# GpSimd's arithmetic in the chunk steps moves to VectorE, and the later blocks of T are placed by DMA

## The chip, the cores and the metric

The kernel runs on one core of a Trainium2 chip. Five engines work side by side, each with its own instruction queue: TensorE (PE in the profile, its weight loads PEld), VectorE (DVE), ScalarE (ACT), GpSimd (POOL) and SyncE (SP), which here only issues DMAs. The metric is the device time of one execution in microseconds (us); lower is better. The kernel before takes 1076.54 us, the median of three runs (1076.4 to 1076.81).

## The reference

The input goes through three layers. The first is a delta-rule attention over 768 tokens for 4 batches of 8 heads with a head size of 48. For each token

```
y[t]   = q[t] @ state
state += beta[t] * outer(k_n[t], v[t] - k_n[t] @ state)        # k_n = k / (|k| + 1e-6)
```

The second is a mixture of 8 experts (384 to 1024 to 384, ReLU). Each of the 3072 tokens goes to the expert with the largest gate logit and is scaled by its softmax weight and by a sigmoid gate. The third is a gated layer, (sigmoid(x @ w_gate) * (x @ w_val)) @ w_out with a width of 1536. Every layer needs the whole output of the one before.

## The kernel before

The attention works on chunks of 32 tokens. A chunk of all 32 pairs of batch and head is one step, so there are 24 steps (`NSTEP`), numbered s. Four steps form a group g (s4 = s % 4), two steps a pair u (s2 = s % 2). The recurrence inside a chunk is solved with a triangular inverse T, one 32x32 matrix for each batch, head and chunk.

A step in program order, with the tiles that the profile names:

1. `KS` = K · state (32 matmuls) on TensorE, then VectorE makes `W` = scaled V minus KS (line 780). `Y` = Q · state follows `KS` on TensorE (line 796).
2. `U` = T · W, 32 matmuls that read `TBD` (line 805). ScalarE rounds `U` to float16 (`UH[:,0]`, line 807), VectorE subtracts to get the low part (`UH[:,1]`, line 811).
3. TensorE fills the time until `UH` is there with the transpose of an earlier output (`XTP`) and with the Gram and Q·K products of step s + 11 (`GP`; up to step 12), then updates the state (`Sps`, 48 matmuls, line 844: high·high, low·high, high·low), and ScalarE copies it to `SH` for the next step's `KS`.
4. TensorE adds the part of the output inside the chunk (`Y` from `PBD`, line 849), the gate logits (`GL`) and the rest of `GP`.

Work for later steps runs beside it. `KH` is the normalised K of a later pair as float16 high and low part (`kh_mul` and `kh_split_hi` on ScalarE, `kh_split_lo` on GpSimd), which four DMAs place in `KBD` (`kexp`). `P` is the masked Q·K product of a later pair: `p_split` scales it and masks it on GpSimd, ScalarE rounds it (`p_split_hi`), GpSimd subtracts for the low part (`p_split_lo`), and four DMAs place it in `PBD` (`expand`). `v_mul` scales V on GpSimd. T of group g + 1 is made while group g runs: `prep` makes norms and the scaled Gram matrix `Lt` (two multiplications over 128x1024 on GpSimd in `scale`, line 341), `inv_ops` runs 31 columns of a multiplication (`tmp<-X,Lt`) and an addition (`X<-X,tmp`) on VectorE, a share of which GpSimd takes (`tmpG`, rows from `SHE[g]` on; `share_rows`). `last` turns X into `XT`, and `expand_t` copies it into `TBD`: the block of step s4 = 0 at once, the blocks of the three later steps in step s4 = 0 of the group, two by VectorE behind the low part of `UH`, two by ScalarE (lines 379 to 385, 813, 874).

Each engine's instructions run in the order of the program text; inside the attention the class `Queue` chains them so. Where the work for later steps goes on VectorE is set by `Filler`: it holds VectorE's side work as pieces with an estimated duration and issues pieces up to a budget at two places of a step: `TA` (2.4) between `W` and the low part of `UH`, and `TB` (4.2; `TC` = 3.8 from step 12 on) at the end of a step. At the end of a group, lines 910 to 912 issue whatever of the next T is still missing, ahead of the next `W`.

GpSimd also scatters each step's tokens to their experts by an indirect DMA (`scatter`). SyncE's queue holds, per step, the loads of later K, Q and V and the four-DMA placements.

Of the kernel before, what the change touches and what calls it, by code (L numbers as in the profile page):

```python
# [7 lines left out]
F32 = mybir.dt.float32  # L8
# [5 lines left out]
ALU = mybir.AluOpType  # L14
# [7 lines left out]
NSTEP, NG = SEQ // CH, SEQ // CH // 4  # L22
# [12 lines left out]
LA = 11  # L35
# [9 lines left out]
XE = (0, 1, 2, 3, 4, 5)  # L45
TB0 = 3.5
# [1 line left out]
WG = 2.7  # L48
WP = 4.5
WE = 1.0  # L50
TC = 3.8
NR = 8
Q2 = 0.0
GS = 6
KA = 1
SHE = (0, 32, 24, 20, 20, 20)
TA = 2.4
TB = 4.2
W0 = 36
YS = 69  # L60
QS = 11
# [34 lines left out]
GAP = 0.12  # L96


class Filler:
# [26 lines left out]
    def run(self, budget):  # L126
        self.t = max(self.t, self.until)
        self.until += budget
        while (self.main or self.chains) and self.t < self.until:
            self.step()  # L130

    def flush(self, chain):
        while chain[1]:
            self.step()
# [6 lines left out]
class Attention:  # L141
# [5 lines left out]
    def run(self, small, acc, zero_fill, small_loads):  # L147
# [42 lines left out]
            return ins.ins  # L190

        def load_kth(u):
            t = wk.tile([128, 2, 48, 8], F32, tag="kth", name="kth", bufs=1)
            SP.dma_start(out=t.rearrange("p s d h -> p s (d h)"), in_=a["ktok"][:, 2 * u : 2 * u + 2])
            KTOK[u] = t

# [2 lines left out]
            SP.dma_start(out=t, in_=a["vtok"][:, 2 * u : 2 * u + 2])  # L199
            VT[u] = t  # L200

        def v_mul(s):
            g, s4 = divmod(s, 4)
            v = VT[s // 2][:, s % 2].rearrange("p (h e) -> p h e", h=8)
            G.tensor_tensor(out=v, in0=v, in1=nt[:, g, 8 * s4 : 8 * s4 + 8].unsqueeze(2).to_broadcast([128, 8, 48]), op=ALU.mult)


        GPS = {}
# [64 lines left out]

        PMS = {}

        def p_split(u):
            g, i = divmod(u, 2)
            if g:
                pm = GPM[g][1][:, 16 * i : 16 * i + 16]
                G.tensor_tensor(out=pm, in0=pm, in1=rnt[:, g, 16 * i : 16 * i + 16].unsqueeze(2).to_broadcast([128, 16, 32]), op=ALU.mult)  # L280
            else:
                pm = PM.pop(u)
            G.tensor_tensor(out=pm, in0=pm, in1=mask.unsqueeze(1).to_broadcast([128, 16, 32]), op=ALU.mult)
# [6 lines left out]
        def p_split_lo(u):  # L290
            G.tensor_tensor(out=PHL[u][:, 1], in0=PMS.pop(u), in1=PHL[u][:, 0], op=ALU.subtract)

        def expand(dst, src):
            for b in range(4):
# [1 line left out]


        def kh_mul(u, half=None):
            r = rnt[:, u // 2].rearrange("p (s h) -> p s h", s=4)
            for i in (range(2) if half is None else (half,)):  # L300
                kt = KTOK[u][:, i]
                if u == 0 or KA:
                    for h in range(8):
                        A.activation(out=kt[:, :, h], in_=kt[:, :, h], func=AF.Copy, scale=r[:, 2 * (u % 2) + i, h : h + 1])
                    continue
                G.tensor_tensor(out=kt, in0=kt, in1=r[:, 2 * (u % 2) + i].unsqueeze(1).to_broadcast([128, 48, 8]), op=ALU.mult)
# [6 lines left out]
                A.copy(out=KH[:, s, 0], in_=by_head(KTOK[u][:, s]))  # L313
            KHG[u] = KH

        def kh_split_lo(u):
            KH, src = KHG[u], KTOK.pop(u)
            for s in range(2):
                G.tensor_tensor(out=KH[:, s, 1], in0=by_head(src[:, s]), in1=KH[:, s, 0], op=ALU.subtract)


        def kexp(u):
# [7 lines left out]
        def prep(g):  # L330
            Lt = ep.tile([128, 32, 32], F32, tag="Lt", name="Lt", bufs=2)
            L1 = Lt.rearrange("p c a -> p (c a)")
            x, y, t, q = [ep.tile([128, 32], F32, tag=n, name=n, bufs=1) for n in ("bx", "by", "bt", "bq")]
            LT[g] = Lt
            R = R0 if g < 2 else R2
            tt = lambda o, a, b: (0.1, GAP, lambda: V.tensor_tensor(out=o, in0=a, in1=b, op=ALU.mult))
            ts = lambda o, a, s1, s2, op1=ALU.add: (0.085, GAP, lambda: V.tensor_scalar(out=o, in0=a, scalar1=s1, scalar2=s2, op0=ALU.mult, op1=op1))
            st = lambda o, a, s1, b, op0=ALU.add: (0.1, GAP, lambda: V.scalar_tensor_tensor(out=o, in0=a, scalar=s1, in1=b, op0=op0, op1=ALU.mult))
            tr = lambda o, i, d: (d, 0.0, lambda: V.transpose(out=o, in_=i))

            def scale(E, j0, j1, i0):
                L = Lt[:, j0:j1, i0:]
                E.tensor_tensor(out=L, in0=L, in1=x[:, j0:j1].unsqueeze(2).to_broadcast([128, j1 - j0, 32 - i0]), op=ALU.mult)
                E.tensor_tensor(out=L, in0=L, in1=nbr[:, g, i0:].unsqueeze(1).to_broadcast([128, j1 - j0, 32 - i0]), op=ALU.mult)


            ops = [
                (1.135, GAP, lambda: V.transpose(out=L1, in_=GPM[g][0].rearrange("p b c -> p c b"))),
                (0.085, GAP, lambda: V.tensor_scalar_max(out=x, in0=L1[:, 0:1024:33], scalar1=1e-36)),
                ts(y.bitcast(I32), x.bitcast(I32), -0.5, 1595932665.0),  # L350
                tt(t, y, y),
                tt(t, t, x),
                st(y, t, -2.38924456, y),
                tt(t, y, y),
                tt(t, t, x),
                ts(q, t, 0.375 * RS**4, -1.25 * RS**2),
                tt(q, q, t),
                st(y, q, 1.875, y),
                tt(y, y, x),
                ts(y, y, -RS / KSC, 1e-6 / KSC),  # L360
                (0.27, GAP, lambda: V.reciprocal(out=x, in_=y)),
                st(nbr[:, g], x, -1.0 / (KSC * KSC), be[:, g], ALU.mult),
                tr(rnt[:, g], x, 0.1),
                tr(nt[:, g], y, 0.1),
            ]
            sc = [(0.0, 0.0, lambda: scale(G, R, 32, R))]
            if R:
                sc.append((R / 12.0, 0.0, lambda: scale(V, 0, R, 0)))
            return ops, sc

        XTS, others = {}, []

# [6 lines left out]
        def expand_t(g, bs, ks):  # L379
            for E, b in zip((V, V, A, A), range(4)):  # L380
                if b in bs:
                    r = slice(32 * b, 32 * b + 32)
                    src = XTS[g][r].rearrange("p i b -> p (i b)").rearrange("p (i b) -> p i b", b=32)
                    dst = TBD[g % 2][r, b % 2].rearrange("p (i b) -> p i b", b=32)
                    (E.copy if E is A else E.tensor_copy)(out=dst[:, :, ks], in_=src[:, :, ks])

        def inv_ops(g, share=32):

# [236 lines left out]
        load_kth(0)  # L625
        load_v(0)
        SP.dma_start(out=be, in_=a["beta"])
        SHz = wk.tile([128, 2, 384], F32, tag="SH", name="SH", bufs=2)
        V.memset(SHz.rearrange("p b c -> p (b c)"), 0.0)
        zap_off(A, KB[4])  # L630
        zap(V, TBD[0], 2)
# [118 lines left out]
        SH = None  # L750
        for s in range(NSTEP):
# [10 lines left out]
            if 0 < s < NSTEP - 1:  # L762
                fill(QB[(s + 1) % 2], s + 1, 1, 64 if s == 1 else 48)
            beside(s, "load", engines)
            if s2 == 0 and 0 < s < NSTEP - 2:
                kh_split_lo(u + 1)
            if s2 == 1 and u + 3 < NSTEP // 2:
                p_split(u + 3)
            if s > 0:
                W = wk.tile([128, 8, 48], F32, tag="W", name="W", bufs=1)  # L770
            UH = wk.tile([128, 2, 8, 48], F16, tag="UH", name="UH", bufs=2)
# [14 lines left out]
            if s2 == 0 and 0 < s < NSTEP - 2:  # L786
                expand(PBD[(u + 1) % 2], PHL.pop(u + 1))
                if half:
                    load_kth(u + 2)
                kexp(u + 1)  # L790

            Yp = pp.tile([128, 8, 48], F32, tag="Y", name="Y")
            ny = NY if s >= LS else 16
# [16 lines left out]
                p_split_lo(s + 1)  # L810
            V.tensor_tensor(out=UH[:, 1], in0=Up, in1=UH[:, 0], op=ALU.subtract)
            if s4 == 0 and g in XE:
                expand_t(g, (0, 1), slice(8, 32))
            beside(s, "U", engines, Sps[1])

            if s > 0:
# [19 lines left out]
                    scatter(w)  # L836

            if not last:
                SH = wk.tile([128, 2, 384], F32, tag="SH", name="SH", bufs=2)
# [19 lines left out]
                for w in range(NSTEP - 8, NSTEP - 4):  # L859
                    scatter(w)  # L860
            if s + 2 < NSTEP and s:
                v_mul(s + 2)
            x_evac(s, Yp)
            if s > 4 and s4 == 1:
                fil.flush(v1)
            if s > 0:
# [3 lines left out]
                    v2 = fil.add(gate_e(g - 1) + gate_v2(g - 1), WE)  # L870
                if s4 == 0:
                    v1 = fil.add(gate_v1(g - 1), WG)
            if s4 == 0 and g in XE:
                expand_t(g, (2, 3), slice(8, 32))
            if s2 == 1 and u + 3 < NSTEP // 2:
                p_split_hi(u + 3)
                p_split_lo(u + 3)
            if more and s:
                gp_mm(s + LA, H8[GS:], mm)
                gp_evac(s + LA)  # L880
# [635 lines left out]
```

## Time and profile before

| what | value |
|---|---|
| median of three runs | 1076.54 us |
| profiled execution | 1079.49 us, of which the trace spans 1077.8 us |
| TensorE busy | 1022.6 us (95%) |
| VectorE busy | 569.2 us (53%) |
| ScalarE busy | 416.9 us (39%) |
| GpSimd busy | 430.2 us (40%) |
| mean granted TensorE clock | 0.898 of full speed |

The trace has four stages: preparation up to 66 us, the chunk steps from 66 to 344, the experts up to about 615, the last layer up to the end. A row of the stage view gives, for one stretch, each engine's busy time and instruction count, the granted TensorE clock (1.0 is 2.4 GHz, 0.5 is 1.2 GHz, a value between them a mix over time), the busy share of the DMA engines and their GB/s. A row of the view by groups gives an operation's tiles and shape, its count, then busy time in us and the mean of one in ns, and behind a second bar the idle time of its engine just before it. Line L87 is a helper through which all of the attention's instructions go, so the tiles tell what an instruction is.

### The profile page before, as it was taken

How to read it: one execution, taken by the hardware profiler on the slowest of the kernel's cores; microseconds unless marked ns; L12 is line 12 of the kernel's file. 1: busy time of each engine (PE TensorE's matmuls, PEld its weight loads, DVE VectorE, ACT ScalarE, POOL GpSimd, SP SyncE). 2: the span in 40 equal slices, each digit the busy share in tenths (PEclk: the TensorE clock that was granted, in tenths of full speed). 3: DMA queues.
4: the chain of work that ended last, by engine and by line, in shares of the span. 5: the costliest groups of instructions: out<-in, count | busy, mean ns of one | idle time of the engine just before them, and what ended most of it. 6: DMA issues, size and time to landing. Idle time of an engine off the chain costs nothing. (4 is left out here: it accounts for less than half of the span.)

```text
span 1077.8 us, 22538 instructions
## 1 busy us (share of the span) xinstructions
PE 1022.6 (95%) x9111; PEld 926.5 (86%) x9112; DVE 569.2 (53%) x1376; ACT 416.9 (39%) x892; POOL 430.2 (40%) x460
## 2 busy tenths in 40 slices
PE   8788999997899999899899899999999999999997
PEld 8777989897898988789889888888888888888886
DVE  6978899989965587667673364511211211211211
ACT  6644646474563444454445232311212222212111
POOL 8455456665733235444444134322322311321322
PEclk8976865566569999999999999999999999999999
DMA  7899977644485365455643222000000000000000
GB/s 187 200 175 201 193 151 142 141 92 86 88 160 133 126 208 155 150 160 171 181 117 117 46 60 74 23 23 1 18 12 1 30 1 1 30 1 1 30 1 30
DMA packets 162622, 100.11 MB, mean 93 GB/s; under 512 B 108025, under 2 KB 152002, under 8 KB 162514
## 3 DMA queue, kind: packets, MB, share of 16 engines
q1 hardware_dynamic: 159442, 89.17, 35.8%
q0 software_dynamic: 3072, 9.46, 2.4%
q8 instruction: 73, 1.20, 0.5%
q14 instruction: 35, 0.29, 0.1%
HBM read 74.94 MB, written 15.80 MB: 84 GB/s over the span
## 5 line engine op out<-in xcount | busy, mean ns | idle before, releaser
L1437 DVE TENSOR_TENSOR gf<-gf,g 128x512 f32<-128x512 f32 x72 | 49.5, 688 | 312.0 <-PE g L1429 310.3
L938 POOL TENSOR_TENSOR gsl<-gf,gsh 128x512 fp32r<-128x512 f32 x68 | 88.7, 1305 | 272.1 <-ACT gsh L937 272.1
L1436 ACT ACTIVATE gf<-g 128x512 f32<-128x512 f32 x72 | 43.0, 597 | 190.8 <-PE g L1429 188.8
L937 ACT CAST gsh<-gf 128x512 fp32r<-128x512 f32 x69 | 42.8, 620 | 144.4 <-DVE gf L1437 142.5
L87 DVE TENSOR_TENSOR X<-X,tmp 128x60 f32<-128x60 f32 (+25 forms) x282 | 96.1, 367 | 1.2
L87 DVE TENSOR_TENSOR tmp<-X,Lt 128x60 f32<-128x60 f32 (+25 forms) x282 | 94.7, 362 | 1.9
L1403 PE MATMUL o<-woh,gsl 128*128 128x384 f32 x272 | 87.3, 339 | 0.0
L1403 PE MATMUL o<-wol,gsh 128*128 128x384 f32 x272 | 86.5, 337 | 0.0
L1118 DVE SCALAR_TENSOR_TENSOR hl<-h,hh 128x460 fp32r<-128x460 f32 (+7 forms) x57 | 33.1, 580 | 61.6 <-ACT hh L1117 61.4
L1429 PE MATMUL g<-yl,wgh 128*128 128x512 f32 x216 | 62.6, 395 | 0.0
L1429 PE MATMUL g<-yl,wvh 128*128 128x512 f32 x216 | 62.3, 395 | 0.0
L1077 PE MATMUL y<-hh,w2h 128*128 128x460 f32 (+6 forms) x168 | 60.8, 362 | 1.2 <-ACT hh L1117 1.0
L1403 PE MATMUL o<-woh,gsh 128*128 128x384 f32 x272 | 61.7, 337 | 0.0
L1429 PE MATMUL g<-yh,wgh 128*128 128x512 f32 x180 | 61.0, 395 | 0.0
L1077 PE MATMUL y<-hh,w2l 128*128 128x460 f32 (+6 forms) x168 | 58.6, 349 | 0.0
L87 ACT ACTIVATE kth<-kth,rnt 128x48 f32<-128x48 f32 x192 | 54.8, 375 | 6.9 <-DMA kth<-in_ktok_dram 6.6
L87 PE MATMUL GP<-KT,KB 112*64 112x64 f32 x640 | 47.8, 315 | 10.2 <-POOL KH L87 7.0
L87 PE MATMUL U<-W,TBD 64*64 64x48 f32 x768 | 47.9, 292 | 8.5 <-DVE W L87 8.5
L87 PEld LDWEIGHTS GP<-KT,KB 112*64 112x64 f32 x640 | 42.6, 221 | 14.7 <-POOL KH L87 7.1
L1403 PEld LDWEIGHTS o<-woh,gsh 128*128 128x128 f32 x272 | 49.7, 188 | 5.8
L87 PEld LDWEIGHTS U<-W,TBD 64*64 64x64 f32 x768 | 44.4, 200 | 10.6 <-DVE W L87 9.2
L1055 POOL TENSOR_TENSOR w1l<-w1r,w1h 128x768 fp32r<-128x768 f32 x19 | 37.2, 1957 | 39.9 <-ACT w1h L1050 39.6
(330 smaller groups left out, 2490.4 us busy)
## 6 DMA issues: line engine op xcount, KB each, us to landing
w1r<-in_w_dram SPq DMA_DIRECT2D x32, 384.0 KB
w2r<-in_w_dram SPq DMA_DIRECT2D x32, 384.0 KB
KT<-in_st_dram SPq DMA_DIRECT2D x20, 448.0 KB
disp<-TBD SPq DMA_DIRECT2D x8, 772.0 KB
kth<-in_ktok_dram SPq DMA_DIRECT2D x12, 384.0 KB
VT<-in_vtok_dram SPq DMA_DIRECT2D x12, 384.0 KB
KBD<-KH SPq DMA_DIRECT2D x48, 96.0 KB
XG<-in_m2g_dram SPq DMA_DIRECT2D x12, 384.0 KB
```

Of the source, the lines that this page charges most:

```text
L87: r = f(*args, **kw)
L937: (act or nc.scalar).copy(out=hi, in_=src)
L938: eng.tensor_tensor(out=lo, in0=src, in1=hi, op=ALU.subtract)
L1055: engine.tensor_tensor(out=l, in0=self.raw[b][i], in1=h, op=ALU.subtract)
L1077: self.T.matmul(out=ys[c][:, 0:n], lhsT=w2[l][:, f % 2, 128 * c : 128 * c + 128], rhs=(hh, hl)[r], start=(f == 0 and i == 0), stop=(f == 7 ...
L1118: self.V.scalar_tensor_tensor(out=hl, in0=hp[:, 0:n], scalar=0.0, in1=hh, op0=ALU.max, op1=ALU.subtract)
L1403: T.matmul(out=ops_[m][:, 0:384], lhsT=gh[l][:, 128 * m : 128 * m + 128], rhs=wo[r][:, f], start=(f == 0 and i == 0), stop=(f == 11 and i ...
L1429: T.matmul(out=ps, lhsT=gv[w][l][:, c, 128 * f : 128 * f + 128], rhs=Y[r][c], start=(i == 0 and c == 0), stop=(i == 2 and c == 2))
L1436: A.activation(out=gf, in_=gps[0], func=AF.Sigmoid)
L1437: V.tensor_tensor(out=gf, in0=gf, in1=gps[1], op=ALU.mult)
```

## The change

VectorE instead of GpSimd now does, from step 1 or 2 on, `kh_split_lo`, `p_split`, `p_split_lo` and `v_mul`. The first two stand right behind the low part of `UH`, `v_mul` behind the state's matmuls, `p_split_lo` after a filler run of `TP` (2.5) at the end of the odd steps. The Filler is told of their time with `spend`. GpSimd's share of the inverse is gone (`SHE` is 32 for groups 1 to 5), and for groups 2 to 5 the scaling of `Lt` is done by VectorE in six pieces that cover 704 of the 1024 elements of a row (the upper blocks of the triangle). The copies of T's later blocks (two on VectorE, two on ScalarE per group) become four DMAs on SyncE's queue, `expand_rest`, in step s4 = 0. `kexp` moves from the middle of an even step to its end. The tile `kth` gets two buffers, `SH` one. The budgets become `TB` 5.8 and `TC` 4.4, and the time given to `spend` counts inside them. `norms` makes sure that a group's norms have been issued before they are read. In step 0 and in the preparation GpSimd keeps these operations.

```diff
-TC = 3.8
+TC = 4.4
-SHE = (0, 32, 24, 20, 20, 20)
+SHE = (0, 32, 32, 32, 32, 32)
-TB = 4.2
+TP = 2.5
+TB = 5.8
...
+    def spend(self, dur):
+        self.t = max(self.t, self.until) + dur
...
-            t = wk.tile([128, 2, 48, 8], F32, tag="kth", name="kth", bufs=1)
+            t = wk.tile([128, 2, 48, 8], F32, tag="kth", name="kth", bufs=2)
...
-            sc = [(0.0, 0.0, lambda: scale(G, R, 32, R))]
             if R:
-                sc.append((R / 12.0, 0.0, lambda: scale(V, 0, R, 0)))
+                sc = [(0.0, 0.0, lambda: scale(G, R, 32, R)), (R / 12.0, 0.0, lambda: scale(V, 0, R, 0))]
+            else:
+                sc = [(0.1 + (j1 - j0) * (32 - i0) / 1200.0, GAP, lambda f=f, r=(j0, j1, i0): f(V, *r))
+                      for f in (by_row, by_col) for j0, j1, i0 in ((0, 8, 0), (8, 16, 8), (16, 32, 16))]
...
+        def expand_rest(g):
+            for b in range(4):
+                r = slice(32 * b, 32 * b + 32)
+                SP.dma_start(
+                    out=TBD[g % 2][r, b % 2].rearrange("p (i b) -> p i b", b=32)[:, :, 8:32],
+                    in_=XTS[g][r].rearrange("p i b -> p (i b)").rearrange("p (i b) -> p i b", b=32)[:, :, 8:32])
...
-            if s2 == 0 and 0 < s < NSTEP - 2:
-                kh_split_lo(u + 1)
-            if s2 == 1 and u + 3 < NSTEP // 2:
-                p_split(u + 3)
...
                 if half:
                     load_kth(u + 2)
-                kexp(u + 1)
...
             V.tensor_tensor(out=UH[:, 1], in0=Up, in1=UH[:, 0], op=ALU.subtract)
             if s4 == 0 and g in XE:
-                expand_t(g, (0, 1), slice(8, 32))
+                expand_rest(g)
+            if s2 == 0:
+                if 0 < s < NSTEP - 2:
+                    kh_split_lo(u + 1, V)
+                    fil.spend(0.95)
+            elif u + 3 < NSTEP // 2:
+                p_split(u + 3, V)
+                fil.spend(1.2)
...
             if s + 2 < NSTEP and s:
-                v_mul(s + 2)
+                v_mul(s + 2, V)
+                fil.spend(0.48)
...
-            if s4 == 0 and g in XE:
-                expand_t(g, (2, 3), slice(8, 32))
             if s2 == 1 and u + 3 < NSTEP // 2:
                 p_split_hi(u + 3)
-                p_split_lo(u + 3)
+                fil.run(TP)
+                p_split_lo(u + 3, V)
+                fil.spend(0.6)
...
+            if s2 == 0 and 0 < s < NSTEP - 2:
+                kexp(u + 1)
             beside(s, "end", engines)
-            fil.run(((TB if s + 1 + LA < NSTEP else TC) - (0.94 if s4 == 0 and g in XE else 0.0)) if s else TB0)
+            fil.run(((TB - (TP if s2 == 1 and u + 3 < NSTEP // 2 else 0.0) if s + 1 + LA < NSTEP else TC)) if s else TB0)
```

## Rows read from the trace of the kernel before

**Rows 1.** The page, part 1: busy us, share of the span, instructions.

```profile
PE 1022.6 (95%) x9111; PEld 926.5 (86%) x9112; DVE 569.2 (53%) x1376; ACT 416.9 (39%) x892; POOL 430.2 (40%) x460
```

**Rows 2.** Stage view: chunk steps; experts; then step 21 alone.

```profile
66.00:344.00 278.00, 255.76 (x4654) 240.71 (x4652) 236.49 (x711) 151.23 (x372) 149.96 (x201) 0.67 0.73 144
344.00:615.00 271.00, 256.94 (x1557) 238.18 (x1555) 171.49 (x316) 126.25 (x239) 108.47 (x71) 0.98 0.46 140
...
322.30:331.30 9.00, 9.00 (x193) 8.53 (x193) 5.55 (x23) 5.28 (x11) 2.83 (x3) 1.00 0.74 177
```

**Rows 3.** Timeline of TensorE (start, us, instruction): step 3, nearly all at full clock.

```profile
104.50 2.11 PE L87 MATMUL KS<-SH,KB 128*64 128x48 f32 x32
...
115.36 2.07 PE L87 MATMUL KS<-SH,KB 128*64 128x48 f32 x32
```

**Rows 4.** Timeline of TensorE: step 8, at half clock, from KS to KS.

```profile
165.47 2.10 PE L87 MATMUL KS<-SH,KB 128*64 128x48 f32 x32
...
169.42 2.01 PE L87 MATMUL U<-W,TBD 64*64 64x48 f32 x32
...
178.02 2.10 PE L87 MATMUL KS<-SH,KB 128*64 128x48 f32 x32
```

**Rows 5.** Waits in the chunk steps: who waited for whom, us, times, longest.

```profile
PE Sps L87 <- DVE UH L87: 12.9, 6, 5.3
...
PE U L87 <- DVE W L87: 8.5, 5, 2.7
```

**Rows 6.** Timeline of VectorE at the end of step 10.

```profile
204.63 2.70 DVE L87 TENSOR_TENSOR tmp<-X,Lt 128x80 f32<-128x80 f32 x2
207.26 1.45 DVE L87 TENSOR_TENSOR X<-X,tmp 128x80 f32<-128x80 f32 x2
```

**Rows 7.** Timeline of GpSimd, same stretch.

```profile
206.20 1.04 POOL L87 TENSOR_TENSOR P<-P,rnt 128x512 f32<-128x512 f32 x1
207.31 1.30 POOL L87 TENSOR_TENSOR P<-P,mask 128x512 f32<-128x512 f32 x1
```

**Rows 8.** Groups on VectorE in the chunk steps.

```profile
L87 DVE TENSOR_TENSOR tmp<-X,Lt 128x90 f32<-128x90 f32 (+34 forms) x226 | 81.0, 384 | 1.6
L87 DVE SCALAR_TENSOR_TENSOR W<-VT,KS 128x384 f32<-128x384 f32 x23 | 12.7, 551 | 15.4 <-PE KS L87 6.0 <-issue 4.6 <-POOL tmpG L87 2.0
```

**Rows 9.** Line L87 on VectorE, chunk steps: ns min/median/max of one.

```profile
L87 DVE TENSOR_TENSOR tmp<-X,Lt x226: 173/260/1869, 70.8 to 306.8; 128x80 f32<-128x80 f32 x8, 128x60 f32<-128x60 f32 x7, 128x90 f32<-128x90 f32 x5, 128x70 f32<-128x70 f32 x5
```

**Rows 10.** Groups on GpSimd in the chunk steps.

```profile
L87 POOL TENSOR_TENSOR KH<-kth,KH 128x384 f16<-128x384 f32 x20 | 23.0, 1172 | 29.9 <-ACT KH L87 24.8 <-DMA KB<-in_st_dram 3.5 <-DMA QB<-in_st_dram 1.7
...
L87 POOL TENSOR_TENSOR VT<-VT,nt 128x384 f32<-128x384 f32 x22 | 20.2, 919 | 0.5
L87 POOL TENSOR_TENSOR PHL<-P,PHL 128x512 f16<-128x512 f32 x10 | 13.6, 1360 | 55.0 <-ACT PHL L87 55.0
L87 POOL TENSOR_TENSOR P<-P,mask 128x512 f32<-128x512 f32 x10 | 13.2, 1320 | 0.8
...
L87 POOL TENSOR_TENSOR P<-P,rnt 128x512 f32<-128x512 f32 x10 | 11.1, 1113 | 0.0
L87 POOL TENSOR_TENSOR Lt<-Lt,nbr 128x1024 f32<-128x1024 f32 x4 | 9.8, 2460 | 0.7 <-DVE g_pos L87 0.6
```

**Rows 11.** Groups on VectorE by shape, 0 to 470 us.

```profile
L87 DVE COPY TBD<-XT 32x768 f32<-32x768 f32 x12 | 8.1, 671 | 0.1
...
L87 DVE TENSOR_TENSOR w1l<-w1r,w1h 128x768 fp32r<-128x768 f32 x2 | 1.9, 954 | 0.1
```

**Rows 12.** Groups on ScalarE in the chunk steps.

```profile
L87 ACT CAST KH<-kth 128x384 f16<-128x384 f32 x20 | 17.1, 904 | 0.0
```

**Rows 13.** Timeline of ScalarE: end of step 7.

```profile
164.78 0.61 ACT L87 CAST PHL<-P 128x512 f16<-128x512 f32 x1
```

**Rows 14.** Timeline of SyncE's queue in step 8.

```profile
173.76 4.17 SPq L87 DMA_DIRECT2D KBD<-KH  x4
```

**Rows 15.** DMA view, 173.7 to 181 us: packets by size.

```profile
DMA packets 4587, 1.38 MB, mean 188 GB/s; under 512 B 4319, under 2 KB 4322, under 8 KB 4585
```

More of the change, by code (lines that the diff above doesn't have):

```diff
@@ L200, in load_v, with v_mul @@
             VT[u] = t
-        def v_mul(s):
+        def v_mul(s, E=G):
             g, s4 = divmod(s, 4)
+            norms(g)
             v = VT[s // 2][:, s % 2].rearrange("p (h e) -> p h e", h=8)
-            G.tensor_tensor(out=v, in0=v, in1=nt[:, g, 8 * s4 : 8 * s4 + 8].unsqueeze(2).to_broadcast([128, 8, 48]), op=ALU.mult)
+            E.tensor_tensor(out=v, in0=v, in1=nt[:, g, 8 * s4 : 8 * s4 + 8].unsqueeze(2).to_broadcast([128, 8, 48]), op=ALU.mult)
         GPS = {}
@@ L274, in run, with p_split @@
         PMS = {}
-        def p_split(u):
+        def p_split(u, E=G):
             g, i = divmod(u, 2)
             if g:
+                norms(g)
                 pm = GPM[g][1][:, 16 * i : 16 * i + 16]
-                G.tensor_tensor(out=pm, in0=pm, in1=rnt[:, g, 16 * i : 16 * i + 16].unsqueeze(2).to_broadcast([128, 16, 32]), op=ALU.mult)
+                E.tensor_tensor(out=pm, in0=pm, in1=rnt[:, g, 16 * i : 16 * i + 16].unsqueeze(2).to_broadcast([128, 16, 32]), op=ALU.mult)
             else:
                 pm = PM.pop(u)
-            G.tensor_tensor(out=pm, in0=pm, in1=mask.unsqueeze(1).to_broadcast([128, 16, 32]), op=ALU.mult)
+            E.tensor_tensor(out=pm, in0=pm, in1=mask.unsqueeze(1).to_broadcast([128, 16, 32]), op=ALU.mult)
             PHL[u] = wk.tile([128, 2, 16, 32], F16, tag="PHL", name="PHL", bufs=4)
@@ L288, in p_split_hi, with p_split_lo @@
             A.copy(out=PHL[u][:, 0], in_=PMS[u])
-        def p_split_lo(u):
-            G.tensor_tensor(out=PHL[u][:, 1], in0=PMS.pop(u), in1=PHL[u][:, 0], op=ALU.subtract)
+        def p_split_lo(u, E=G):
+            E.tensor_tensor(out=PHL[u][:, 1], in0=PMS.pop(u), in1=PHL[u][:, 0], op=ALU.subtract)
         def expand(dst, src):
@@ L298, in kh_mul @@
         def kh_mul(u, half=None):
+            norms(u // 2)
             r = rnt[:, u // 2].rearrange("p (s h) -> p s h", s=4)
@@ L314, in kh_split_hi, with kh_split_lo @@
             KHG[u] = KH
-        def kh_split_lo(u):
+        def kh_split_lo(u, E=G):
             KH, src = KHG[u], KTOK.pop(u)
             for s in range(2):
-                G.tensor_tensor(out=KH[:, s, 1], in0=by_head(src[:, s]), in1=KH[:, s, 0], op=ALU.subtract)
+                E.tensor_tensor(out=KH[:, s, 1], in0=by_head(src[:, s]), in1=KH[:, s, 0], op=ALU.subtract)
         def kexp(u):
@@ L339, in prep, with by_row, by_col, scale @@
             tr = lambda o, i, d: (d, 0.0, lambda: V.transpose(out=o, in_=i))
-            def scale(E, j0, j1, i0):
+            def by_row(E, j0, j1, i0):
                 L = Lt[:, j0:j1, i0:]
                 E.tensor_tensor(out=L, in0=L, in1=x[:, j0:j1].unsqueeze(2).to_broadcast([128, j1 - j0, 32 - i0]), op=ALU.mult)
+            def by_col(E, j0, j1, i0):
+                L = Lt[:, j0:j1, i0:]
                 E.tensor_tensor(out=L, in0=L, in1=nbr[:, g, i0:].unsqueeze(1).to_broadcast([128, j1 - j0, 32 - i0]), op=ALU.mult)
+            def scale(E, *r):
+                by_row(E, *r)
+                by_col(E, *r)
             ops = [
@@ L365, in prep, with norms @@
             ]
-            sc = [(0.0, 0.0, lambda: scale(G, R, 32, R))]
             if R:
-                sc.append((R / 12.0, 0.0, lambda: scale(V, 0, R, 0)))
-            return ops, sc
+                sc = [(0.0, 0.0, lambda: scale(G, R, 32, R)), (R / 12.0, 0.0, lambda: scale(V, 0, R, 0))]
+            else:
+                sc = [(0.1 + (j1 - j0) * (32 - i0) / 1200.0, GAP, lambda f=f, r=(j0, j1, i0): f(V, *r))
+                      for f in (by_row, by_col) for j0, j1, i0 in ((0, 8, 0), (8, 16, 8), (16, 32, 16))]
+            return ops + [(0.0, 0.0, lambda: normed.add(g))], sc
+        normed = set()
+        def norms(g):
+            while g not in normed:
+                fil.step()
         XTS, others = {}, []
@@ L627, in run @@
         SP.dma_start(out=be, in_=a["beta"])
-        SHz = wk.tile([128, 2, 384], F32, tag="SH", name="SH", bufs=2)
+        SHz = wk.tile([128, 2, 384], F32, tag="SH", name="SH", bufs=1)
         V.memset(SHz.rearrange("p b c -> p (b c)"), 0.0)
@@ L838, in run @@
             if not last:
-                SH = wk.tile([128, 2, 384], F32, tag="SH", name="SH", bufs=2)
+                SH = wk.tile([128, 2, 384], F32, tag="SH", name="SH", bufs=1)
                 for p, i in ((0, 0), (0, 1), (0, 2), (1, 0), (1, 1), (1, 2)) if s < LS or not SP2 else ((0, 0), (0, 1), (1, 0), (1, 1), (0, 2), (1, 2)):
```

## The prediction

> **What bounds the kernel now.** The page gives TensorE 95% of the span as busy and VectorE 53% [rows 1], an average over stages with different limits, so I went to the stage view. The experts and the last layer run TensorE at full clock or nearly (0.98 in the experts, 257 of 271 us busy) and the change touches nothing there. The chunk steps take 278 us with TensorE at a mean granted clock of 0.67, VectorE busy 236.5 us and GpSimd 150 us [rows 2]. Every microsecond that this stage loses or gains moves the end, because the experts need all of its tokens.
>
> Next I read one step from KS to KS on TensorE's timeline. Step 3, nearly all at full clock (2.4 GHz), took 115.36 − 104.50 = 10.86 us [rows 3]. Step 8, at half clock (1.2 GHz), took 178.02 − 165.47 = 12.55 us with no gap over 0.4 us between matmuls [rows 4]. A late step without GP takes 9.0 us at full clock [rows 2]. So half clock costs 1.69 us, 13.5% of a half-clock step. A mean of 0.67 is 66% of the time at half clock, 183 us; at full clock all along these would be 25 us shorter.
>
> The second loss is in the view of waits: the state's matmuls waited 12.9 us for the low part of UH and U's matmuls 8.5 us for W, both made by VectorE [rows 5]. That is 21.4 us of TensorE standing still, in 11 waits.
>
> Why VectorE is late stands in two timelines. At the end of step 10 a pair of tmp<-X,Lt pieces takes 2.70 us and the next pair 1.45 us [rows 6]. The first ends at 207.33, where GpSimd's P<-P,rnt ends (207.24), the second at 208.71, where P<-P,mask ends (208.61) [rows 7]: VectorE's instruction stands until GpSimd's is through. For the whole stage, the 226 tmp<-X,Lt have a mean of 384 ns [rows 8] and a median of 260 [rows 9], so 28 us lie above the median. There are 226 additions X<-X,tmp of the same shapes; taken alike, some 56 us of VectorE's time is waiting on GpSimd.
>
> **The change, part by part.** The sum is made against the profiled execution, 1079.49 us (span 1077.8); the median of the runs shown is 1076.54, 2.95 lower, and the same difference is taken from it.
>
> *What VectorE gets.* Dense 128x384 costs 0.55 us there (W, [rows 8]), 128x768 costs 0.95 [rows 11], so 128x512 lies between; I take 0.68. Counts come from GpSimd's rows [rows 10], less those that step 0 or 1 keeps: 20 KH at 0.55 = 11.0; 21 of 22 VT = 11.6; 9 of 10 PHL = 6.1; 9 each of P<-P,mask and P<-P,rnt = 12.2. Lt: four groups of six pieces of 192 or 256 elements, from the median of 0.26 to W's 0.55 each, I take 0.38: 9.1. GpSimd's share of X goes into pieces that exist already: 40 multiplications at 0.30 on GpSimd with as many additions, bounded by 24 us there and zero; a few elements more per piece, I take 2. Sum 52. Off goes VectorE's half of the copies to TBD, 12 at 0.67 = 8 [rows 11]. Net +44 us.
>
> Bounds of that price: below, KH and P by overlap with the next instruction, some 40; above, GpSimd's own durations, 23.0 + 19.3 + 12.2 + 11.9 + 10.0 and, for Lt, four times two at up to 2.46 = 19.7 and 24 for X [rows 10], in all 120. KH is the doubtful one: it reads K with a stride between elements, and ScalarE needs 0.90 us for that 128x384 [rows 12] against 0.61 for a dense 128x512 [rows 13]; at that price KH costs 18 instead of 11. I stay with the dense row, the nearest on the same engine.
>
> The Trainium skill (Perfetto Trace Analysis, Optimizing Scalar/DVE Operations) says that moving work between GpSimd and VectorE might not help, since the two share a read port of SBUF. By it the total would be 1079, no change; rows 6 and 7 agree that the two hold each other up, but the prices, 0.55 us on VectorE against 0.92 on GpSimd for 128x384, speak for a gain.
>
> *What goes.* With no GpSimd arithmetic beside it, the 56 us of waiting goes, but for what scatter's indirect DMAs still cause (they stay). VectorE's work is then 236.5 + 44 − 56 = 224.5 us, a little less than before; what matters more is that no piece ahead of W or of UH grows to 2 us. Of the 21.4 us of waits I leave 4: the first two fall in steps 1 and 2, behind operations that GpSimd keeps. Gain 17.4 us. What is late next is TensorE itself, at 10.86 or 12.55 us a step.
>
> *The clock.* Steps without waits exist at either level [rows 3, 4], so the waits alone don't set it. I take 5 of the 25 us back, a fifth, for a TensorE that stands still less. Ends: the whole 25 back; or half clock through the 95 us that now run at full, 95 × 1.69 / 10.86 = 15 us lost.
>
> *Where the new pieces stand.* In even steps kh_split_lo waits for ScalarE's KH and then stands between the low part of UH and the filler run; from there to W TensorE has some 6 us of work, and v_mul, kh_split_lo and the filler are budgeted 5.8: hidden. In odd steps p_split_lo waits for ScalarE's rounding of P, with the filler and W queued behind it. In step 7 that rounding ended at 165.39 [rows 13]; 0.68 for the subtraction, 2.7 of filler and 0.55 for W end at 169.3, and U began at 169.42 when nothing held it [rows 4]. So it just fits at half clock; at full clock both sides move up together. If it misses by 0.5 us, 9 odd steps cost 4.5. From step 12 on the budget is 2.4 + 4.4 = 6.8 a step with about 7.4 a group for the moved pieces, 19.8 left where there was 4 × 6.2 − 0.94 = 23.9, and Lt and X add 2.8 a group (six pieces at 0.38, and 0.5): up to 7 us of T's pieces are issued ahead of the next group's first W in steps 15 and 19. Some 1 us of that is hidden behind Y; earlier groups' spare time takes more. I put +2.4 for all of these, with 0 and 12 as the ends.
>
> *SyncE.* The four DMAs of T have the form of KBD's: 32 partitions, runs of 96 B, 4096 packets for the four. KBD's took 4.17 us to issue [rows 14], and of the packets under 512 B in its stretch 4319 had started by 181 [rows 15], 7.3 us after the first issue. T's take KBD's place in the queue, at 173.76, so they land at about 181; the next U begins 12.55 us after this step's, at 181.97, or 10.86 after, at 180.3. At half clock it is hidden, at full clock it may cost 0.7 us in the two groups whose K loads stand ahead: 0 to 2 us, I take 0. KBD follows at 178 to 182 and is read a step later; behind it in the queue stand the next step's K loads, read 11 steps later, and its Q load, read in the step after. The other buffers (kth 2, SH 1) cost nothing: ScalarE writes SH only after matmuls that stand behind SH's last reader in TensorE's queue.
>
> [...]
>
> **Sum.** −17.4 − 5 + 2.4 = −20.0: the profiled execution 1059.5, the median 1056.5 us.
>
> **Rivals.**
> A. *The clock stays down.* Waits go, but TensorE remains at half clock or goes there altogether, as step 8 for it. −17.4 + 2.4 + (0 to 15): −15 to 0, so 1061.5 to 1076.5 in the median. Against it: steps 3 and 21 hold full clock without waits [rows 2, 3].
> B. *VectorE becomes the bound, slower.* Place: W, at the end of each step. Now it is busy 236.5 of 278 us, so about 41.5 us of unavoidable waiting on its own. If that stays, the stage takes 224.5 + 41.5 = 266: still 12 less. It turns slower once the moved work costs over 64 instead of 52 us, as with KH at 0.90 and 0.3 us more for each P. At 80 us the stage takes 294: +16, median 1092. For it: the pieces stand in W's queue, and 120 is the upper bound. Against: VectorE's prices per element.
> C. *T's DMAs land late.* Should the four take 14 us, twice KBD's time, steps 1, 5, 9 and so on wait some 7 us each, 6 × 7 = 42, median 1098; it cancels the gain from 3.3 us per group. KBD's rows speak against.
> D. *No gain*, VectorE's and GpSimd's shared time is only handed over: 1076.
>
> **How the numbers follow.** The forecast with −10 to −35: 0.68. A, beyond that but faster by over 0.2%: 0.13. D and what else ends within 0.2% (about what a measurement tells from no change): 0.06. Slower: B 0.10, C 0.03. Faster is thus 0.81, same 0.06, slower 0.13. The range reaches from −35 (all 21.4 us of waits and 14 of clock), 1041, to −3.5, 1073, where most of A is inside and B, C and D are left out.
>
> **What would show it.** Right: tmp<-X,Lt with a mean near its median; PE's waits for UH and W below 6 us together; chunk steps of 252 to 262 us; clock over 0.67. Wrong: U waiting for a DMA of TBD in steps 5 and 9 (C); VectorE without idle time ahead of W and waits of TensorE on W that grow in odd steps or in steps 15 and 19 (B); a clock near 0.5 without waits (A).

## The result: 1.35% slower, because T's pieces end up ahead of W

The changed kernel takes 1092.45 us, the median of four runs (1091.35 to 1095.12), against 1076.67 us for the kernel before on the same chip. The ratio is 1.0135, with a 95% interval of 1.0102 to 1.0168. The forecast was 1056.5 us and its range 1041 to 1073: wrong, and on the other side. The profiled execution took 1095.12 us, the slowest of the four, with a span of 1093.4.

The page first (answers to [rows 1]): GpSimd gave up 116 us of busy time, VectorE did not become busier.

```profile
PE 1031.5 (94%) x9111; PEld 933.7 (85%) x9112; DVE 546.1 (50%) x1428; ACT 406.7 (37%) x880; POOL 314.0 (29%) x304
```

The stage view, chunk steps and then experts (answers to [rows 2]; the stage has slid to about 60 to 360). The experts take the same 271 us as before; the chunk steps lost all of it, with VectorE idle for 83 of their 300 us and the granted clock at 0.56 in this execution.

```profile
60.00:360.00 300.00, 268.88 (x4716) 251.96 (x4713) 216.79 (x774) 140.76 (x360) 34.33 (x45) 0.56 0.72 144
360.00:631.00 271.00, 257.72 (x1560) 239.06 (x1558) 169.89 (x312) 125.89 (x238) 108.26 (x71) 0.97 0.47 140
```

From the first U of step 0 to the last of step 23 it is 278.6 us before and 296.8 after. I split both. TensorE's gaps, counted wherever a matmul starts more than 0.4 us after the one before it, are 24.6 and 34.0 us. The second part is half clock, 184.3 and 262.8 us of it, of which each microsecond costs 0.135 [rows 3, 4], so 24.9 and 35.5. The remainder is 229.1 and 227.3: the work itself is the same. So this pair of profiles shows +9.4 us of gaps and +10.6 of clock. Going by the means of more runs of its neighbours, told below, 3 to 5 us of the second number are of the kernel, and the rest is the luck of the two executions.

The groups of TensorE after (busy us, mean ns, then its idle time just before them with its causes; answers to [rows 5]): the state's matmuls no longer wait for UH, 12.9 us there went to 0.1 in all; U waits 22.8 us for W instead of 8.5, and 4.4 for a DMA of TBD.

```profile
L88 PE MATMUL U<-W,TBD 64*64 64x48 f32 x758 | 47.9, 304 | 27.2 <-DVE W L88 22.8 <-DMA TBD<-XT 4.4
L88 PE MATMUL Sps<-UH,KBD 64*128 64x48 f16 x1104 | 41.6, 207 | 0.1
```

TensorE's timeline after: where U waited for W longest, and one step inside a group. The long waits for W stand at the first step of a group and nowhere else (in the kernel before, none of the five did): steps 8, 12, 16 and 20, together 21.5 of the 22.8 us. A step without a wait at half clock takes 207.05 − 194.45 = 12.60 us, as before [rows 4].

```profile
172.91 2.01 PE L88 MATMUL U<-W,TBD 64*64 64x48 f32 x32 [3.20 <-DVE W L88]
...
194.45 2.10 PE L88 MATMUL KS<-SH,KB 128*64 128x48 f32 x32
...
207.05 2.10 PE L88 MATMUL KS<-SH,KB 128*64 128x48 f32 x32
...
226.68 2.02 PE L88 MATMUL U<-W,TBD 64*64 64x48 f32 x32 [4.80 <-DVE W L88]
...
278.78 2.01 PE L88 MATMUL U<-W,TBD 64*64 64x48 f32 x32 [7.60 <-DVE W L88]
...
327.04 2.01 PE L88 MATMUL U<-W,TBD 64*64 64x48 f32 x32 [5.90 <-DVE W L88]
```

VectorE's timeline ahead of the third of them, the end of step 15. From 268.20 on nothing but T's pieces runs, then T's transposition (`XT`) and the copies of its first block, and only then W. K · state, which W needs, was ready at about 269 (KS started at 267.12, Y follows at 269.04). The pieces are short, none is held up by another engine: there are simply ten microseconds of them in the wrong place. By the program's own estimate 4.3 us of them are what the budgets had left over; the others belong to the step's own budget. This is what "issue whatever of the next T is still missing, ahead of the next W" looks like.

```profile
268.20 0.40 DVE L88 TENSOR_TENSOR X<-X,tmp 128x240 f32<-128x240 f32 x1
268.64 0.47 DVE L88 TENSOR_TENSOR tmp<-X,Lt 128x110 f32<-128x110 f32 x2
...
275.38 0.21 DVE L88 TENSOR_TENSOR X<-X,tmp 128x31 f32<-128x31 f32 x1
275.62 1.90 DVE L88 STREAM_TRANSPOSE XT<-X 128x1024 f32<-128x1024 f32 x1
277.56 0.58 DVE L88 COPY TBD<-XT 32x256 f32<-32x256 f32 x2
278.17 0.55 DVE L88 SCALAR_TENSOR_TENSOR W<-VT,KS 128x384 f32<-128x384 f32 x1
```

And yet VectorE has time. In the view of waits after, it is VectorE that waits inside the steps: for ScalarE's half of UH, for ScalarE's rounding of P, for KS.

```profile
DVE UH L88 <- ACT UH L88: 39.8, 21, 5.2
...
DVE PHL L88 <- ACT PHL L88: 17.4, 9, 3.0
DVE W L88 <- PE KS L88: 17.0, 10, 4.1
```

What the change was made for did happen. VectorE's groups after (answers to [rows 8, 10]) and the spread of one of them ([rows 9]): T's multiplications have a mean of 286 ns, near their median of 267 where it was 384 against 260, and none above 421 where the longest took 1869.

```profile
L88 DVE TENSOR_TENSOR tmp<-X,Lt 128x31 f32<-128x31 f32 (+29 forms) x217 | 56.9, 286 | 1.4
L88 DVE TENSOR_TENSOR KH<-kth,KH 128x384 f16<-128x384 f32 x20 | 16.0, 840 | 0.0
L88 DVE TENSOR_TENSOR UH<-U,UH 128x384 f16<-128x384 f32 x23 | 12.8, 558 | 38.5 <-ACT UH L88 38.2
...
L88 DVE TENSOR_TENSOR VT<-VT,nt 128x384 f32<-128x384 f32 x21 | 11.5, 547 | 0.0
...
L88 DVE TENSOR_TENSOR P<-P,mask 128x512 f32<-128x512 f32 x9 | 7.1, 788 | 0.3
L88 DVE TENSOR_TENSOR PHL<-P,PHL 128x512 f16<-128x512 f32 x9 | 6.2, 692 | 17.4 <-ACT PHL L88 17.4
L88 DVE TENSOR_TENSOR P<-P,rnt 128x512 f32<-128x512 f32 x9 | 6.1, 682 | 0.0
L88 DVE TENSOR_TENSOR Lt<-Lt,bx 128x256 f32<-128x256 f32 (+1 forms) x12 | 4.7, 395 | 0.0
L88 DVE TENSOR_TENSOR Lt<-Lt,nbr 128x256 f32<-128x256 f32 (+1 forms) x12 | 4.7, 394 | 0.0
```

```profile
L88 DVE TENSOR_TENSOR tmp<-X,Lt x217: 177/267/421, 59.9 to 323.4; 128x31 f32<-128x31 f32 x6, 128x87 f32<-128x87 f32 x6, 128x255 f32<-128x255 f32 x6, 128x60 f32<-128x60 f32 x6
```

### The profile page after: what moved, and what is told of

The parts are those of the page before. It is cut to its first block, busy times and chain, and to the rows that moved or that the text cites. A ratio compares the mean times of both kernels' runs of the same rounds, so it can differ in the third digit from the quotient of the medians.

```text
span 1093.4 us, 22430 instructions
## 1 busy us (share of the span) xinstructions
PE 1031.5 (94%) x9111; PEld 933.7 (85%) x9112; DVE 546.1 (50%) x1428; ACT 406.7 (37%) x880; POOL 314.0 (29%) x304
## 5 line engine op out<-in xcount | busy, mean ns | idle before, releaser
L88 PE MATMUL U<-W,TBD 64*64 64x48 f32 x768 | 48.5, 304 | 27.2 <-DVE W L88 22.8
L88 DVE TENSOR_TENSOR tmp<-X,Lt 128x84 f32<-128x84 f32 (+33 forms) x268 | 71.7, 292 | 1.6
L88 DVE TENSOR_TENSOR X<-X,tmp 128x84 f32<-128x84 f32 (+33 forms) x268 | 71.9, 292 | 1.1
L88 POOL COPY XG<-g_sc 128x2 f32<-128x2 f32 x24 | 6.6, 273 | 207.8 <-DVE g_sc L88 196.8
```

What stands on the lines that cost most here:

```text
L88: r = f(*args, **kw)
```

## The experiments

Theory F: the change's budgets are too small for the work that it gave to VectorE, so what is left of T stands ahead of W at each group's end, while VectorE idles earlier in the steps. Rival B: VectorE has too much work, wherever it stands. Rival C: the DMAs of T are late. Each ratio below is to the kernel before, run beside it on the same chip, with its 95% interval.

**More of T ahead of UH.** The changed kernel with one constant changed.

```diff
-TA = 2.4
+TA = 4.2
```

> The changed kernel with one constant altered: the budget TA, between W and the low part of UH, is 4.2 instead of 2.4, so that the pieces of T's inverse that were forced ahead of W at the ends of groups 1 to 4 are spread over the steps (counted in the program's own estimate, 1.9 + 2.6 + 4.3 + 3.2 us were forced, now 0). Theory F (the lateness comes from pieces left over and forced ahead of W): TensorE's four waits for W of 3.5, 5.1, 7.9 and 6.2 us go, some 22 us, minus up to 4 us for a later UH; time 1068 to 1076 if the clock stays as it is, down to 1055 if it comes up. Rival B (VectorE has too much work altogether): the waits only move to UH and to W within the steps, time 1085 to 1092. Rival C (the DMA of T's blocks is late): no change but for the waits that it names, 1085 to 1090.

Measured: 1082.76 us, 0.9999 (0.9973 to 1.0025). One constant takes back all of the loss; the work on VectorE is the same, so B falls as its cause. F's 1068 to 1076, set against the 1076.5 of the kernel before, was missed by a little all the same (the kernel before takes 1082.14 us on this chip); T's DMAs, seen below, are in the way. The waits of U after it are 3.8 us for W, and the rest is for the DMAs of T. The view puts one wait of 4.1 us down to `tmp`, but U reads only W and TBD: in that step, step 1, W had ended at 72.77 and U's two parts began at 77.11 and 78.94.

```profile
PE U L88 <- DVE tmp L88: 4.1, 1, 4.1
PE U L88 <- DVE W L88: 3.8, 4, 1.5
...
PE U L88 <- DMA TBD<-XT: 3.4, 3, 1.4
```

```profile
72.22 0.55 DVE L88 SCALAR_TENSOR_TENSOR W<-VT,KS 128x384 f32<-128x384 f32 x1
```

```profile
77.11 0.43 PE L88 MATMUL U<-W,TBD 64*64 64x48 f32 x2 [4.10 <-DVE tmp L88]
78.94 1.97 PE L88 MATMUL U<-W,TBD 64*64 64x48 f32 x30 [1.40 <-DMA TBD<-XT]
```

The end of T tells it as well. In the changed kernel its transposition starts at 169.73, 223.52, 275.62 and 323.88, each time 3.2 us before the U that reads it. With TA 4.2 the T's of groups 2 to 5 are transposed at 148.79, 186.09, 231.24 and 280.00, where the U's that need them start at 171.70, 223.56, 273.02 and 315.52: VectorE is 23 to 42 us ahead instead of never catching up. VectorE's wait for ScalarE's rounding of P, which stands right ahead of the pile, is much the same in both (17.4 us in the changed kernel, 14.8 here), so that wait doesn't make the loss.

**More at the end of the step instead.** The changed kernel with larger budgets at the other place.

```diff
-TC = 4.4
+TC = 6.6
-TB = 5.8
+TB = 7.4
```

> The changed kernel with the other two budgets raised instead: TB 7.4 for 5.8, TC 6.6 for 4.4, so that the same pieces stand between UH and the next W. Theory F with VectorE's room where I took it to be (some 6 us between UH and W): no forced pieces, 1070 to 1078. If the room is ahead of UH (VectorE waited 38 us there for ScalarE in the changed kernel), W is late by about 1 us in many steps instead: 1078 to 1092, slower than with TA raised. Rival B: 1085 to 1095.

Measured: 1089.86 us, 1.0069 (1.0046 to 1.0091). The pile at the group's end is gone, but U waits for W in ten smaller pieces, 17.2 us in all, the longest 3.5, while VectorE still idles 32.3 us ahead of UH, as the second reading of the expectation said. Of the two places, the budget does better between W and UH, where TensorE's U covers it.

```profile
PE U L88 <- DVE W L88: 17.2, 10, 3.5
```

**The arithmetic alone.** The changed kernel with TA 4.2 and T's copies back on VectorE and ScalarE: the DMAs are undone.

```diff
-TA = 2.4
+TA = 4.2
...
-                expand_rest(g)
+                expand_t(g, (0, 1), slice(8, 32))
+                fil.spend(0.94)
...
+            if s4 == 0 and g in XE:
+                expand_t(g, (2, 3), slice(8, 32))
```

> The arithmetic part alone, with TA at 4.2: T's later blocks are copied by VectorE and ScalarE as before the change (0.94 counted for them), no forced pieces. Against the run with TA 4.2 and the DMAs it tells what the DMAs are worth when nothing is forced. Theory F: within 5 us of that run, 1068 to 1078. Rival C: faster than it by 5 us or more. Rival B: 1085 to 1095 as that one.

Measured: 1076.24 us, 0.9941 (0.9910 to 0.9973): faster than the kernel before. It ran beside the first experiment, from which it differs in how T's later blocks are placed, and in the 0.94 counted for that; means of ten runs each differ by 6.3 us. That is C's sign in this expectation: the DMAs do cost something, if not the loss.

**The DMAs alone.** The kernel before with T placed by DMA, `kexp` at the end, and the buffers as changed.

```diff
-                kexp(u + 1)
...
-                expand_t(g, (0, 1), slice(8, 32))
+                expand_rest(g)
...
-            if s4 == 0 and g in XE:
-                expand_t(g, (2, 3), slice(8, 32))
...
+            if s2 == 0 and 0 < s < NSTEP - 2:
+                kexp(u + 1)
-            fil.run(((TB if s + 1 + LA < NSTEP else TC) - (0.94 if s4 == 0 and g in XE else 0.0)) if s else TB0)
+            fil.run(((TB if s + 1 + LA < NSTEP else TC)) if s else TB0)
```

> The kernel before with only the DMA part of the change: T's later blocks by four DMAs, KBD's DMAs at the end of the even steps, two buffers of kth, one of SH; GpSimd keeps its arithmetic, and the 0.94 that was taken off the budget for the copies is given back. Theory F: 8 us less on VectorE and 14 less on ScalarE, the same or slightly faster, 1068 to 1078, with waits for TBD's DMAs below 5 us. Rival C: slower, 1080 to 1095, with waits of several us for TBD in steps 5, 9 and so on.

Measured: 1091.37 us, 1.0071 (1.0038 to 1.0105). It came out where C had put it and not F, but it isn't a clean test: U waits 5.2 us for T's DMAs (four waits), but also 12.1 us for W, behind pieces that GpSimd's arithmetic still stretches (a pair of 128x80 took 2.79 us at 152.35). The DMA's part is best seen in one step. SyncE's queue and TensorE's timeline in step 8 and 9:

```profile
174.00 1.26 SPq L87 DMA_DIRECT2D PBD<-PHL  x1
175.30 1.42 SPq L87 DMA_DIRECT2D kth<-in_ktok_dram  x1
176.84 5.06 SPq L87 DMA_DIRECT2D TBD<-XT  x4
```

```profile
183.02 0.42 PE L87 MATMUL U<-W,TBD 64*64 64x48 f32 x2
184.85 2.00 PE L87 MATMUL U<-W,TBD 64*64 64x48 f32 x30 [1.41 <-DMA TBD<-XT]
```

The first two matmuls of U could start, the other 30 waited: 184.85 − 176.84 = 8.0 us after the first of the four was issued, and that issue had the placement of P and the load of kth ahead of it in the queue.

**The forced pieces, with the arithmetic and without the DMAs.** As the arithmetic alone, but with TA 2.4 and nothing put down for the copies, so that what is left for the group's end is the same as in the changed kernel.

```diff
-TA = 4.2
+TA = 2.4
...
-                fil.spend(0.94)
```

> The changed kernel with only its DMAs for T undone: T's blocks are copied by VectorE and ScalarE as before the change, budgets as in the changed kernel and the copies not counted in them, so that the same pieces are forced. Theory F: the forced pieces stay dear, 1085 to 1093, within 5 us of the changed kernel; the DMAs cost what they did with TA 4.2, some 6 us. Rival C: below 1080, most of the loss is the DMAs'.

Measured: 1091.07 us, 1.0103 (1.0054 to 1.0152), against 0.9941 for the same arithmetic with TA 4.2. U waits 24.1 us for W (eight waits, the longest 7.6), as in the changed kernel (22.8, 7.6). By the two ratios the DMAs add only 0.3% on top of this, and the intervals overlap. That the DMAs cost less here because W, late by up to 7.6 us, leaves them the time to land fits the changed kernel's waits (none for T's DMAs from step 2 on), but is an argument, not a test.

**The forced pieces alone.** The kernel before, nothing moved, with smaller budgets.

```diff
-TC = 3.8
+TC = 3.4
-TB = 4.2
+TB = 3.8
```

> The kernel before with nothing but its budgets lowered (TB 3.8 for 4.2, TC 3.4 for 3.8), so that pieces of T are forced ahead of W at the ends of groups 2 to 4: 2.0, 4.6 and 4.7 us by the program's own estimate, 11.3 in all, against 12.1 in the changed kernel. Theory F: slower than the kernel before by 6 to 12 us without any operation moved to another engine, with waits of 3 us and more for W at these places. If the forced pieces do no harm by themselves: within 3 us of it.

Measured: 1098.65 us, 1.0180 (1.0129 to 1.0231). 0.4 us less per step in the budgets of the old kernel costs as much as the whole change or more (the two intervals overlap): some 19 us where I expected 6 to 12. Its waits for W are 17.8 us longer than the kernel before's, and most of them stands in steps 8, 12, 16 and 20 (2.80, 3.14, 6.95 and 9.55 us); the mean granted clock of its runs is lower by 0.017. Step 8 waits though by the program's estimate nothing was forced ahead of it. The view's row, and the largest wait on TensorE's timeline, step 20:

```profile
PE U L87 <- DVE W L87: 26.3, 7, 9.6
```

```profile
326.03 2.00 PE L87 MATMUL U<-W,TBD 64*64 64x48 f32 x32 [9.55 <-DVE W L87]
```

**A budget between.** The arithmetic alone with less ahead of UH and more at the end.

```diff
-TA = 4.2
+TA = 3.4
-TC = 4.4
+TC = 5.4
-TB = 5.8
+TB = 6.6
```

> The arithmetic part alone (copies of T's blocks as before the change), with the budgets shared out otherwise: TA 3.4, TB 6.6, TC 5.4 for 4.2, 5.8, 4.4; nothing is forced. The run with TA 4.2 still had 8 us of TensorE waiting for W and 8 for UH. Theory F: with less ahead of UH its waits go and W's stay about equal, 1070 to 1076. Rival B (VectorE has too much work altogether): what leaves one wait comes back in the other, 1074 to 1080.

Measured: 1080.35 us, 1.0006 (0.9980 to 1.0033). U waits 13.4 us for W in ten waits, where it waited 6.3 with TA 4.2, and the state's matmuls 0.7 us for UH instead of 4.1: what left one wait came back in the other, and more, as B's reading of this run said. So where the budget stands still matters when nothing is forced, and the arithmetic's gain showed only with more of it ahead of UH.

**More work for TensorE.** The arithmetic alone, with eight matmuls on zeros ahead of U in every step, to see the clock move.

```diff
-            if s == 0:
+            if True:
                 for _ in range(B0):
```

> The arithmetic part alone with TA 4.2, and in every step 8 matmuls of zeros (128x128 by 128, float16, into an unused part of U's bank, as step 0 has them already) between Y and U. If the clock of the chunk steps is what is left to gain (216 of 277 us at half clock in that run), and is raised by a busier TensorE in this place, half clock falls to below 100 us: 16 us gained at a price of 8 x 0.055 to 0.107 us a step, 10 to 20 in all less what waiting hides: 1066 to 1076. If it is not, the price alone shows: 1082 to 1094 with as much half clock as before.

Measured: 1080.60 us, 0.9988 (0.9946 to 1.0030). The mean granted clock of its runs was 0.909 against 0.887 of the same kernel without them (on another chip; the kernel before has 0.890 on both), and half clock in the chunk steps of the profiles was 153.6 us instead of 215.7. So the clock does answer, though half clock doesn't fall below 100 us as the first reading had it, and it costs about what it gives: 62.1 × 0.135 = 8.4 us back, gaps 18.1 to 11.6 us, and yet 2.4 us longer in the chunk steps, so the dummies cost some 17.

**The arithmetic alone, again, and three neighbours.** Four kernels on one chip, each with its own expectation: the same kernel as above; TA 4.6 in it; three matmuls on zeros ahead of U in steps 1 to 11 in it; and the same three in the kernel before, as control.

```diff
-TA = 4.2
+TA = 4.6
```

```diff
-            if s == 0:
-                for _ in range(B0):
+            if s < 12:
+                for _ in range(B0 if s == 0 else 3):
```

> The same kernel as the arithmetic alone with TA 4.2, run again beside more runs of the kernel before, because its gain (0.9941) is small and the times of one kernel scatter by some 0.3% with the granted clock. If the gain is of the kernel: ratio 0.992 to 0.996, with U waiting for W under 8 us and half clock between 200 and 230 us in the chunk steps. If it was the scatter of that chip: ratio 0.997 to 1.002.

> The arithmetic alone, with TA 4.6 instead of 4.2. If what is left of the loss is W waiting behind T's pieces at the end of a step (6.3 us in 8 waits at TA 4.2), more budget ahead of UH takes 2 to 4 us of it: ratio 0.990 to 0.994. If the budget is now at its best, the state's matmuls wait for the low part of UH instead (4.1 us at TA 4.2, then 8 or more): ratio 0.995 to 1.000.

> The arithmetic alone, with three matmuls on zeros ahead of U in steps 1 to 11 (eight in every step cost about 16 us, 0.087 us each, and shortened half clock from 216 to 154 us). Here the price is 33 x 0.087 = 2.9 us. If the half clock is shortened in proportion, by some 12 us, this gives 1.6 back: ratio 0.994 to 0.998. If three are enough for the whole effect (62 us less, 8.4 us back): ratio 0.988 to 0.991. If the clock doesn't answer to them: 0.996 to 1.000.

> The kernel before, with the same three matmuls on zeros in steps 1 to 11: the control for the run above. If the clock answers to them whatever VectorE does, this kernel gains or loses as much against its own base as the other does, within 0.3%. If the moved arithmetic is what pulls the clock down and the dummies only undo that, the kernel before has nothing to gain: ratio 1.001 to 1.004, the price of the dummies alone.

Measured, in this order: 1074.85 us, 0.9914 (0.9883 to 0.9945); 1079.22 us, 0.9940 (0.9920 to 0.9961); 1075.57 us, 0.9912 (0.9880 to 0.9944); 1087.53 us, 1.0017 (0.9985 to 1.0048). The gain of the arithmetic alone is of the kernel. TA 4.6 is no better: U's wait for W stays at 5.9 us and the state's matmuls wait 8.0 us for UH, as its second reading said; its ratio lies on the edge of the first reading. Three matmuls on zeros do nothing that can be told apart, in either kernel: the mean granted clocks with and without them are 0.879 and 0.879, and 0.870 and 0.872 in the kernel before.

```profile
PE Sps L88 <- DVE UH L88: 8.0, 9, 1.8
...
PE U L88 <- DVE W L88: 5.9, 7, 1.5
```

The version that beats both kernels is thus the arithmetic on VectorE with TA 4.2 and T's copies where they were, 0.6 to 0.9% under the kernel before. The new place of `kexp` and the buffers of `kth` and `SH` are in it too and were not tested apart, nor was the budget `TP`.

**The sum of the parts.** Arithmetic with fitting budgets −0.6% (and −0.9% in the second run), DMAs in that kernel +0.6%, budgets +1.35% (from 0.9999 to 1.0135). These add up to the change's 1.35% by the way they are made, each a step from one kernel to the next, and the shares depend on the order: with the short budgets first, the budgets cost 1.6% (0.9941 to 1.0103) and the DMAs 0.3%. In either order the short budgets are the large part.

## Why the prediction was wrong

*What bounds the kernel, and what goes.* Right: tmp near its median, none of its pieces stretched to 2 us, no waits for UH. The price of the moved work was right but for KH: 0.840 us instead of 0.55, nearer to the 0.90 that I had named as its doubtful bound; P<-P,mask had a mean of 0.79 instead of 0.68 (eight of nine took 0.69, one 1.55), VT 0.55, Lt 0.39. That makes some 7 us more in all, and it doesn't decide anything: VectorE is idle for 83 us of the stage. Of the 21.4 us of waits I left 4 for steps 1 and 2, where 8.0 of them stood (2.68 and 5.30); 20.0 went, more than my 17.4.

*The step that failed.* "Up to 7 us of T's pieces are issued ahead of the next group's first W in steps 15 and 19. Some 1 us of that is hidden behind Y; earlier groups' spare time takes more. I put +2.4 for all of these, with 0 and 12 as the ends." Measured: 21.5 us of waits at four group ends. Two things were wrong in it. First, spare time that VectorE has is not spare time that the Filler uses: it issues by its budgets, and what they don't hold waits for the group's end however long VectorE idles. I worked out the budget for the steps from 12 on alone. The same sum for the groups before says 4 × (2.4 + 5.8) − 7.4 = 25.4 where there was 4 × (2.4 + 4.2) − 0.94 = 25.5, with 2.8 more to do: short as well, and steps 8 and 12 waited 3.2 and 4.8 us. Second, the price of a short budget isn't the piece that is missing: by the program's estimate 1.9, 2.6, 4.3 and 3.2 us were left over, and the waits are 1.3 to 3.3 us longer. The pile ends with the transposition (1.90 us), the first copies (0.58) and W (0.55), some 3 us that are hidden when T is ready a step early and stand nearly bare when it is late by anything at all. The estimates hide part of this: they count the transposition as 1.135 us and the copies as nothing. The kernel before with 0.4 us less per step shows the same alone: 1.8%. The term was 21.5 us, far outside its end of 12.

Term by term, in the two profiles: 20.0 us of waits went where I had 17.4; 21.5 came at the group ends where I had 2.4; 4.4 came for T's DMAs and 2.9 for Q's loads where I had nothing for either. That is some +9 us of gaps, as measured (+9.4), where I had −15. The waits of Y for Q's loads stand in steps 4 and 6; the kernel with the forced pieces and without T's DMAs has 3.5 us of them, so T's DMAs are not needed for them, and their cause stays open.

```profile
PE Y L88 <- DMA QB<-in_st_dram: 2.9, 2, 2.0
```

*SyncE.* "I take 0", with 2 as the end: 6.3 us between the two kernels that differ in this. The duration was nearly right: 8.0 us from the first issue to U's rest where I had 7.3. In the DMAs-alone kernel's step 8, which ran at full clock (U at 172.17, the next at 183.02), the issue came 4.7 us after U, about as forecast, and the next U, split in two, ended 1.8 us late instead of 0.7. What I had not seen is steps 0 and 4. With TA 4.2 their U's started at 62.96 and 117.05, but T's DMAs were issued at 70.62 and 124.41, 7.7 and 7.4 us later, in step 4 behind the placement of P and the load of kth, and U of steps 1 and 5 waited 5.5 and 2.1 us for them. In step 1 of the changed kernel U waited 4.4 us for T's DMAs. Its later groups show no such wait; C was right in kind and 6 us, not 42, in size. These waits, 7.5 us against 0.9 for W in step 1 of the kernel with the copies, alone come to about the 6.3; whether the clock (0.879 and 0.887 in the means of ten runs, some 2.5 us by the 0.135 above) adds to it isn't separated.

*The clock.* I took 5 us back. The pair of profiles shows 10.6 us lost, but the profiled execution of the kernel before was at 0.898, and the changed one's at 0.866, while the four runs of the changed kernel go from 0.866 to 0.893, with a mean of 0.880, and 70 runs of the kernel before on three chips have means of 0.890, 0.890 and 0.872. On one chip at a time, the arithmetic alone is within 0.007 of the kernel before, on either side; the kernels with T's DMAs or forced pieces are lower by 0.010 to 0.017, worth 3 to 5 us. So moving the arithmetic shows no effect on the clock beyond that 0.007, and fewer waits for UH gave none of it back that can be seen. Whether the waits for W lower it, as those numbers suggest, was not shown.

*The rivals.* B was named with its place, W, and even with its median of 1092, and was given 0.10 for the wrong reason: I priced too much work and found room for it, where the question was when the Filler lets it run. That its 1092 is the time measured is luck: it came from moved work of 80 us, which cost some 59. A clock near 0.5 without waits (A) describes most of the changed kernel's steps, but not its loss.

The Trainium skill (Perfetto Trace Analysis, Optimizing Scalar/DVE Operations) says that moving work between VectorE and GpSimd might not help, because of the shared read port. Here it did help, by 0.6 to 0.9%, once the budgets let it: the time that T's pieces stood behind GpSimd in [rows 8, 9] is gone, with a mean now 19 ns over the median.

## What to carry to other kernels

Where a program decides when side work is issued, an engine's idle time alone says little: recompute the schedule's budgets with the new work in them, for every stage of the loop and not the last alone, and ask what happens to the remainder and what stands behind it. After such a move tune the budget before judging the move: here one constant was worth 1.35%, more than the move itself at 0.6 to 0.9%, and the place of the budget (ahead of UH, under TensorE's U) mattered as much as its size. And a DMA that takes another's place in a queue starts when those ahead of it are through, not when its data are ready.

## What the runs showed of the hardware

A subtraction of 128x384 with a float16 result takes VectorE 0.56 us for UH, where U is read densely (from PSUM), and 0.84 us for KH, where K is read with a stride of 8 elements (from SBUF). Four DMAs of 32 partitions in runs of 96 B needed 6.4 to 8.3 us from the first issue to the rest of U in the nine places where U waited for them. Executions of one kernel on one chip scatter by about 0.3% (one standard deviation), and part of the scatter goes with the clock (a third to two thirds of the variance, in three sets of runs of the kernel before): among 28 runs of the kernel before, 0.01 of mean granted clock goes with 2 us, among 19 others with 4; 0.01 of 1080 us is 21.6 us more at half clock, which at 0.135 makes 2.9.
